# Loading 16 slots of the last V tile as two pieces of 8 in a decode attention kernel

## The chip, the cores and the metric

One core of a Trainium2 chip. The metric is the device time of one execution, in microseconds (us). The change concerns the last 4 us of some 630.

## The reference

Decode attention with grouped queries: 1 query per head, 32 query heads, 8 K/V heads, 65,536 keys, head size 128, bf16.

```python
k = jnp.repeat(k, rep, axis=1)              # rep = 32 / 8
v = jnp.repeat(v, rep, axis=1)
scores = jnp.einsum("bhqd,bhkd->bhqk", q, k) * D ** -0.5
p = _softmax(scores, axis=-1)
return jnp.einsum("bhqk,bhkd->bhqd", p, v)
```

K and V are 134 MB each and every byte is used once.

## The kernel before

K and V of a head are loaded in two tiles each, of 128 partitions x 256 "slots" (keys) x 128 values: 8 MB. The last V tile of all is loaded in ever smaller pieces, each with its own semaphore, so that little work is left when the last byte lands:

```python
TAIL = 32
CUTS = [0, 128, 192, 224, 240, 248, 252, 256]
...
    # load_v, last tile (SP issues); earlier piece, waits: cut
    for lo, hi, s in list(zip(CUTS, CUTS[1:], s_v))[1:]:
        load(v, g, b, 0, s, lo, hi)
```

TensorE multiplies slots 0 to 223 in groups of four (512 columns) into one accumulator. VectorE folds that accumulator into one row per partition (`vs`) while the last 32 slots arrive. Those are taken slot by slot (128 columns), and the folded part is added by the gather (two matmuls in the trace) before the last piece:

```python
    for t in range(SL - TAIL, SL):                 # slots 224 to 255
        if t in CUTS:
            pe.wait_ge(s_v[CUTS.index(t)], 16)
        if t == CUTS[-2]:                          # slot 252
            pe.wait_ge(s_dv, d_last)               # VectorE's fold is done
            gather(D, start=False, stop=False)
        w0 = t % PS // 4 * 32 + 16 + 4 * (t % 4)
        i = pe.matmul(
            out=fin, lhsT=et[:, 1, w0:w0 + H], rhs=io[:, t, :], start=(t == SL - TAIL),
            stop=(t == SL - 1), skip_group_check=True,
        )
    i.then_inc(s_pe, 1)                            # then ACT scales, and stores the result
```

Of the kernel before, what the change touches and what calls it, by code (L numbers as in the profile page):

```python
# [21 lines left out]
WB = 160  # L22
PS = 64
TAIL = 32
CUTS = [0, 128, 192, 224, 240, 248, 252, 256]


class Queue:
# [21 lines left out]
def kernel(  # L50
# [21 lines left out]
    def sem(name):  # L72
        return ctx.enter_context(nc.semaphore(name))
# [33 lines left out]
    s_q, s_st = sem("s_q"), sem("s_st")  # L107
    s_v = [sem(f"s_v{i}") for i in range(len(CUTS) - 1)]
    s_dv, s_ac, s_gp = sem("s_dv"), sem("s_ac"), sem("s_gp")
# [8 lines left out]
    def down(eng, which, s, n, wait=False):  # L118

        w = dict(sync_type="semaphore", id=s.num, ant_name=s.name)  # L120
        eng.add_instruction(mybir.InstEventSemaphore(  # L121
            name=nc.get_next_instruction_name(), engine=which, sync_info=mybir.SyncInfo(
                on_wait=[mybir.SyncWait(wait_mode="sem-ge-imm", wait_value=n, **w)] if wait else [],
                on_update=[mybir.SyncUpdate(update_mode="sem-sub-imm", update_value=n, **w)],
            ),
        ))
# [11 lines left out]
    def load(src, g, b, at, s, lo=0, hi=SL):  # L138
        sp.dma_start(  # L139
            out=io[:, at * SL + lo:at * SL + hi, :], in_=rows(src, g, b)[:, lo:hi, :]  # L140
        ).then_inc(s, 16)
# [13 lines left out]
    def values_done(n):  # L155
        SP.wait((s_vc, n))
        if n:
            sp.sem_inc(s_vd, 1)  # L158

    def load_v(g, b):  # L160
        done = 2 * (2 * g + b)
        if (g, b) == (G - 1, 1):
            SP.wait((s_vc, done - 1))
            load(v, g, b, 0, s_v[0], CUTS[0], CUTS[1])
            values_done(done)
            down(sp, mybir.EngineType.SP, s_v[2], 16)
            for lo, hi, s in list(zip(CUTS, CUTS[1:], s_v))[1:]:
                load(v, g, b, 0, s, lo, hi)
# [182 lines left out]
    for t in range(SL - TAIL, SL):  # L351
        if t in CUTS:
            pe.wait_ge(s_v[CUTS.index(t)], 16)
        if t == CUTS[-2]:
            pe.wait_ge(s_dv, d_last)
# [200 lines left out]
```

## Time and profile before

| | before |
|---|---|
| time, median of 3 (range) | 629.74 us (629.56 to 630.29) |
| span of the profiled run | 627.6 us |
| DMA queue, share of the 16 engines' span | 99.1% |
| TensorE, VectorE busy | 56%, 55% |

The lines behind this are shown in the prediction. The loads run for 99% of the span, so what is left to win is the time from the last loads to the end.

### The profile page before, as it was taken

Reading aid. Unit: us, or ns where it says so; the run is one execution under the profiler, and the core shown is the slowest. Engines: PE = TensorE matmul, PEld = TensorE weight load, DVE = VectorE, ACT = ScalarE, POOL = GpSimd, SP = SyncE. Lnnn points to the kernel's source line nnn. Section 1 sums busy time; section 2 is a strip of 40 time slices with the busy share of each in tenths; the row PEclk is TensorE's granted clock in tenths of the full one; section 3 lists DMA queues with packets and bytes.
Section 4 is the critical chain, followed back from the end, with each engine's and each line's share of the span. In section 5 each row is a group of like instructions: output and inputs, shape, how many; then the busy total and the mean of one; then the engine's idle time right before and its main releaser. Section 6 shows DMA issues by size and latency. Waiting matters only on the chain. (4 is left out here: it accounts for less than half of the span.)

```text
span 627.6 us, 7061 instructions
## 1 busy us (share of the span) xinstructions
PE 350.0 (56%) x2142; PEld 137.9 (22%) x2142; DVE 345.5 (55%) x154; ACT 34.4 (5%) x26; POOL 8.8 (1%) x40
## 2 busy tenths in 40 slices
PE   1865483827638275381844809458183571886344
PEld 0322131312213032130321303123031230332112
DVE  7795835649066490764807557084670946684210
ACT  0000100020000200002000020000200002000100
POOL 2000000000000000000000000000000000000000
PEclk9979696977959789596896968869698695999578
DMA  8999999999999999999999999999999999999996
GB/s 365 438 468 401 468 401 468 401 468 401 468 401 468 401 468 401 451 418 447 422 418 451 418 451 414 455 405 464 401 468 401 468 401 468 396 440 434 434 434 269
DMA packets 6859, 268.48 MB, mean 428 GB/s; under 512 B 841, under 2 KB 1097, under 8 KB 1353
## 3 DMA queue, kind: packets, MB, share of 16 engines
q1 hardware_dynamic: 6800, 268.45, 99.1%
q8 instruction: 1, 0.02, 0.0%
q10 hardware_dynamic: 56, 0.01, 0.0%
q14 instruction: 2, 0.01, 0.0%
HBM read 268.44 MB, written 0.01 MB: 428 GB/s over the span
## 5 line engine op out<-in xcount | busy, mean ns | idle before, releaser
L300 PE MATMUL acc<-io,wz 128*128 x1024 | 268.1, 412 | 190.0 <-PEq L121 160.3
L372 DVE STREAM_TRANSPOSE io<-io 128x4096 uint32<-128x4096 uint32 x64 | 279.9, 4416 | 157.8 <-DVEq L121 157.8
L300 PEld LDWEIGHTS acc<-io,wz 128*128 x1024 | 104.8, 102 | 353.4 <-issue 273.6
L253 PE MATMUL acc<-io,et 128*16 128x512 bf16 x1016 | 70.9, 409 | 20.4 <-PEq L121 19.3
L439 ACT ACTIVATE zs<-acc,nmb 128x2048 bf16<-128x2048 f32 x8 | 15.7, 1967 | 556.7 <-DVE nmb L419 556.7
L409 DVE TENSOR_REDUCE mg<-acc 128x1 f32<-128x2048 f32 x8 | 18.3, 2292 | 48.3 <-DVEq L121 48.3
L253 PEld LDWEIGHTS acc<-io,et 128*16 128x16 bf16 x1016 | 27.6, 94 | 58.5 <-issue 34.7
L247 PE MATMUL pf<-zs,sel 128*4 128x130 f32 (+1 forms) x20 | 5.7, 387 | 53.3 <-PEq L121 53.3
L375 DVE STREAM_TRANSPOSE et<-zs 128x1024 bf16<-128x1024 bf16 x17 | 20.8, 1225 | 21.9 <-SPq L158 12.1
L449 ACT ACTIVATE acc<-wz 128x2560 f32<-128x2560 bf16 (+2 forms) x8 | 16.3, 2040 | 1.0 <-ACT zs L439 0.2
L411 DVE TENSOR_REDUCE m<-pt 1x4 f32<-1x128 f32 x8 | 2.2, 279 | 22.8 <-DVEq L121 22.8
L518 POOL COPY wz<-qT 32x16 bf16<-32x16 bf16 x32 | 6.1, 189 | 513.4 <-PE acc L300 441.0
L247 PEld LDWEIGHTS pf<-zs,sel 128*4 128x4 f32 x20 | 1.2, 83 | 53.7 <-issue 53.7
L325 PE MATMUL pt<-et 128*16 128x512 bf16 x32 | 12.9, 405 | 0.0
L383 DVE TENSOR_REDUCE zs<-zs 128x128 f32<-128x512 f32 x9 | 6.1, 681 | 7.6 <-DVEq L121 7.6
L422 DVE TENSOR_TENSOR zs<-acc,sely 128x512 f32<-128x512 f32 x8 | 8.5, 1066 | 0.0
L471 DVE TENSOR_TENSOR zs<-acc,sely 128x512 f32<-128x512 f32 x1 | 0.7, 691 | 11.6 <-PE acc L253 11.6
L342 PE MATMUL pb<-ident,nrow 1*128 1x1 f32 x8 | 1.6, 199 | 7.5 <-PEq L121 7.5
L325 PEld LDWEIGHTS pt<-et 128*16 128x16 bf16 x32 | 3.1, 96 | 4.3 <-issue 1.1
L340 PE MATMUL pt<-ident,mg 128*1 128x128 f32 x8 | 2.3, 283 | 2.6 <-PEq L121 2.6
L419 DVE COPY nmb<-pb 128x1 f32<-128x1 f32 x8 | 1.3, 158 | 4.0 <-DVEq L121 4.0
L342 PEld LDWEIGHTS pb<-ident,nrow 1*128 1x128 f32 x8 | 1.2, 144 | 8.9 <-issue 8.9
(29 smaller groups left out, 21.2 us busy)
## 6 DMA issues: line engine op xcount, KB each, us to landing
io<-in_v_dram SPq DMA_DIRECT2D x5, 4096.0 KB, 16.9
io<-in_k_dram SPq DMA_DIRECT2D x8, 2048.0 KB, 27.3
io<-in_k_dram SPq DMA_DIRECT2D x2, 4096.0 KB, 34.3
io<-in_v_dram SPq DMA_DIRECT2D x1, 2048.0 KB, 10.7
io<-in_v_dram SPq DMA_DIRECT2D x1, 1024.0 KB, 12.9
io<-in_v_dram SPq DMA_DIRECT2D x1, 512.0 KB, 13.7
io<-in_v_dram SPq DMA_DIRECT2D x1, 256.0 KB, 13.9
io<-in_v_dram SPq DMA_DIRECT2D x2, 128.0 KB, 13.7
```

The source lines that it names most:

```text
L247: return pe.matmul(out=pf[0:H, 0:w], lhsT=sel[:, :], rhs=vs[:, 0:w], skip_group_check=True, **kw)
L253: return pe.matmul(out=vacc[32 * c:32 * c + 16, :, :], lhsT=et[:, ch // 2, w0:w0 + 16], rhs=io[:, PS * ch + 4 * tt:PS * ch + 4 * tt + 4, : ...
L300: i = pe.matmul(out=bass.AP(acc, r_o, [[2560, P], [1, 512]]), lhsT=bass.AP(wz, r_w + ((2 * s + e) * WB - 4 * u), [[4 * WB, P], [1, P]]), r ...
L325: pe.matmul(out=pt[0:16, :], lhsT=et[:, 0, 0:16], rhs=et[:, 0, :], start=True, stop=True)
L372: dve.transpose(out=part, in_=part).then_inc(s_kt, 2)
L375: dve.transpose(out=et[:, :, :].rearrange("p i n -> p (i n)"), in_=ex[:, 2 * b:2 * b + 2, :].rearrange("p i n -> p (i n)"),).then_inc(s_et, 1)
L383: DV.mark(dve.tensor_reduce(out=vs[:, 0:D], in_=vy[:, :, :], axis=AX.X, op=ALU.add))
L409: dve.tensor_reduce(out=mg[:, :], in_=sc, axis=AX.X, op=ALU.max).then_inc(s_mg, 1)
L422: dve.tensor_tensor(out=vy[:, :, :].rearrange("p d y -> p y d"), in0=vacc, in1=sely[:, :, None].to_broadcast([P, 4, D]), op=ALU.mult,).the ...
L439: act.activation(out=ex[:, :, :].rearrange("p b n -> p (b n)"), in_=sc, func=ACT.Exp, bias=nmb[:, :], scale=SCALE, accum_out=vs[:, D + g % ...
L449: act.activation(out=part, in_=wz[:, 0, 0:1].to_broadcast([P, part.shape[1]]), func=ACT.Copy).then_inc(s_cl, 1)
L518: gp.tensor_copy(out=wz[r, :, c0:c0 + H].rearrange("p (s w) h -> p s w h", s=2), in_=qTb[r, :, :, g, :],).then_inc(s_w, 1)
```

## The change

The intent is to let TensorE begin on slots 224 to 231 when they are there, instead of waiting for all 16.

```diff
-CUTS = [0, 128, 192, 224, 240, 248, 252, 256]
+CUTS = [0, 128, 192, 224, 232, 240, 248, 252, 256]
```

Through the loops above this adds one load, one semaphore and one wait on TensorE.

## The prediction

The sum: 629.74 - 0.13 = 629.61 us, each term from the trace or the runs of the kernel before.

> **What bounds the kernel now.** I read the page from its top down: first the shares of the span, to find the engine that is never idle, then the chain that ended last, to see what sets the end, and then the last microseconds piece by piece, since the change touches nothing else.
>
> The DMA row and the queues, from the page of the kernel before:
>
> ```profile
> span 627.6 us, 7061 instructions
> PE 350.0 (56%) x2142; PEld 137.9 (22%) x2142; DVE 345.5 (55%) x154; ACT 34.4 (5%) x26; POOL 8.8 (1%) x40
> ...
> DMA  8999999999999999999999999999999999999996
> ...
> q1 hardware_dynamic: 6800, 268.45, 99.1%
> ...
> HBM read 268.44 MB, written 0.01 MB: 428 GB/s over the span
> ```
>
> No compute engine is busy for more than 56% of the span, and the DMA row shows nines in nearly every slice. 268.4 MB of K and V are loaded once, by one queue that takes 99.1% of the 16 engines' time. So some 620 of the 627.6 us are the stream of loads, which the change leaves as it is (same bytes, same order, same addresses). Only the tail, from the arrival of the last V slots to the end, can move. Its chain of waits, in order of time (start, us, what):
>
> ```profile
> 608.12 0.43 SPq L139
> 608.55 0.04 issue
> 608.59 13.68 DMA io<-in_v_dram
> 622.27 0.04 issue
> 622.32 1.73 PE pf L358 x28
> 624.04 0.22 PE pf L247 x2
> 624.26 0.24 PE pf L358 x4
> 624.50 0.02 issue
> 624.52 0.02 ACTq L37
> 624.53 0.05 issue
> 624.59 0.36 ACT o L486
> ```
>
> The load issued at 608.59 us is the 16-slot piece (512 KB), the very one that is to be split. When it has landed, at 622.27 us, TensorE runs 28 of the 32 small matmuls of the tail without a stop, then the two gather matmuls, then the last 4. The later pieces (8, 4 and 4 slots) do not appear: their data is there before TensorE asks. So from 622.32 us on TensorE is the bound, and the start of that burst is set by the piece in question. The timeline of that stretch (start, us, engine, line, op, tile, number, idle time before) shows what TensorE did ahead of it, and that VectorE is in time:
>
> ```profile
> 621.02 0.61 PE L253 MATMUL acc<-io,et 128*16 128x512 bf16 x8 [1.15 <-DMA io<-in_v_dram]
> 621.45 0.20 PE L347 MATMUL pb<-zs,sel 128*4 128x1 f32 x2
> 622.32 1.73 PE L358 MATMUL pf<-io,et 128*4 128x128 bf16 x28 [0.66 <-DMA io<-in_v_dram]
> 622.86 0.29 DVE L479 TENSOR_TENSOR zs<-zs 128x128 f32<-128x128 f32 x1
> ```
>
> TensorE stands idle for 0.66 us before the burst; that idle time is what the change can use. VectorE's last sum, which the gather needs, ends at 622.86 + 0.29 = 623.15 us.
>
> From the trace's semaphore and packet records I took what these views merge. The last of the 16 completions of each piece came at 620.972 (slots 192 to 224), 622.271 (224 to 240), 622.959 (240 to 248), 623.317 (248 to 252) and 623.625 us (252 to 256). A packet took 159 ns at 4096 B, 84 ns at 2048 B and 47 ns at 1024 B (medians). The 28 matmuls start from 622.316 to 623.822 us: (623.822 - 622.316) / 27 = 0.0558 us apart.
>
> [...] the pieces complete in the order of their issue. So the two halves arrive one after the other, and the first half comes about half the piece's time earlier. [...] the trace has 16 completions for the 16-slot piece, spread over 0.43 us (621.845 to 622.271), and the split gives this count to each half. [...] two 2048 B packets take 168 ns where one of 4096 B takes 159. [...]
>
> **The change part by part.** The build of both kernels shows one more DMA on SP (the 16-slot piece becomes two of 8, so three 8-slot loads in a row), one more wait on TensorE (8 matmuls, wait, 8 matmuls in place of 16), and nothing else moved on any engine.
>
> *SP issue.* The issues of these pieces start 0.474 us apart (608.591, 609.065, 609.539, 610.013). One more shifts the later three and the store of the first seven groups by 0.47 us. The pieces wait some 13.7 us in the queue from issue to landing, so a later issue delays no data. Cost on the path: 0.
>
> *DMA.* An 8-slot piece takes from the landing of its predecessor 622.959 - 622.271 = 0.688 us (8 packets per engine at 84 ns, and 16 ns). Two of them take 1.376 us, where the 16-slot piece took 622.271 - 620.972 = 1.299. Everything behind is later by 0.077 us. The landings become: first half 620.972 + 0.688 = 621.660; second half 622.348; slots 240 to 248 at 623.036; 248 to 252 at 623.394; 252 to 256 at 623.702.
>
> *TensorE.* A waiting matmul starts 0.045 us after the landing (622.271 to 622.316). First half: start 621.705 (the work ahead of it ends at 621.65, so nothing holds it), 8 x 0.0558, free at 622.15. Second half: start 622.393, free at 622.84. Now TensorE has caught up with the loads, and the next piece, which it never waited for, holds it: start 623.081. The 4 of slots 248 to 252 follow without a wait (landed 623.394, wanted at 623.53). The gather would follow at 623.081 + 12 x 0.0558 = 623.751; its own wait is for slots 252 to 256, free at 623.702 + 0.045 = 623.747, a dead heat, and VectorE's sum has been there since 623.15.
>
> *Sum.* The gather started at 623.877 before, and starts at 623.751 after: 0.126 us sooner. What follows it (two gather matmuls, 4 matmuls, the scaling on ACT, the store) is unchanged. Of the 0.611 us by which the first matmul starts sooner, 0.485 us is given back in waits for the second half and for slots 240 to 248. 629.74 - 0.13 = 629.61 us, or 0.02%.
>
> **The rivals.** First, TensorE stays the bound and the whole 0.61 us is won (629.13 us). For it: before, no wait lies inside the burst. Against it: 8 matmuls take 0.45 us and an 8-slot piece 0.69, so the loads are the slower side as soon as TensorE starts early. It could be so only at half the granted clock, at which a matmul would take about twice 0.0558, or 0.11 us, and 8 of them 0.89 us. The profile gives 0.50 from 613 to 617 us and 1.00 from 618 on, so runs in which the low clock lasts longer would be slower in both kernels, and gain more from the split.
>
> Second, the smaller pieces delay the last landing enough that the gather waits for it and the gain is gone: 629.74 us or a little more. The last landing had 623.823 - 623.625 = 0.2 us to spare before. The computed delay of 0.077 does not use that up. If a split cost 0.3 us in place of 0.077, the gather would start at 623.97, or 0.1 us later than before: 629.84 us.
>
> Third, the extra issue holds up the queue: at worst 0.47 us, so 630.2 us. Against it stand the 13.7 us of queueing. The first 2048 B packet of the tail begins at 621.265 us, 12.2 us after its issue.
>
> Fourth, the gain is real but drowned by the differences between runs: the three of before spread over 0.73 us (629.56 to 630.29), almost six times the gain. This is what I expect of the plain times.
>
> **Range and chances.** The point is 629.6 us. All mechanisms together give 629.1 to 630.2. The spread between runs, and a possible other chip for the changed kernel, which I cannot know, widen it: 629.0 to 630.4. A change of over 2% would be 12.6 us, and the whole tail from the last landing to the end of the span is 627.6 - 623.6 = 4.0 us. So within 2% has 0.99, and the rest is halved between the sides, for something that I do not see.
>
> **What would show it.** In the trace after: matmuls of the tail in three bursts, 8, 8 and 16 with the gather in between, each started by a landing; landings 0.69 us apart three times; the chain of waits passing through a later load, slots 240 to 248 or 252 to 256, in place of the first piece; the gap from the landing of slots 192 to 224 to the gather matmul down from 623.877 - 620.972 = 2.905 us to about 2.78. Wrong would be: a burst of 32 without a wait from the first half on (the first rival), a gather that starts later after that landing than 2.905 us (the second), or a gap between the landings before slots 224 (the third).

## The result, and the profile after

| | before | after |
|---|---|---|
| median of 6 runs | 630.01 us | 629.49 us |
| range | 629.43 to 631.23 | 629.32 to 630.30 |
| ratio | | 0.9991 (95%: 0.9978 to 1.0004) |
| span of the profiled run | 627.6 us | 627.8 us |

Ratios here are the mean time of one kernel's runs over that of the other's in the same rounds, so not quite the ratio of the medians. Executions over 1.5% slower than the fastest of the same kernel are left out of the means. The interval includes 1: timing alone shows no difference. The spread of each kernel's own runs is several times the predicted gain of 0.13 us.

The page of the kernel after, DMA row and load queue. The stream of loads is as before; the queue has 144 packets more (128 for the split, 16 for its completions):

```profile
DMA  8999999999999999999999999999999999999996
...
q1 hardware_dynamic: 6944, 268.45, 99.1%
```

The end of its chain of waits (start, us, what):

```profile
608.60 12.41 DMA io<-in_v_dram
621.00 0.04 issue
621.05 1.02 PE acc L253 x5
622.07 0.02 PE pb L347
622.10 1.84 PE pf L358 x28
623.94 0.32 PE pf L247 x2
624.26 0.24 PE pf L358 x4
```

This is not the predicted chain: it runs through the load that ends at 621.00, which is slots 192 to 224, and then stays on TensorE. The windows of the same trace (columns: window, its length, busy time of PE, PEld, DVE, ACT, POOL, then granted clock, DMA share, GB/s) tell why TensorE was behind at first. The granted clock is the share of TensorE's full clock that the profile records:

```profile
620.50:622.00 1.50, 1.40 (x16) 0.38 (x12) 0.00 (x0) 0.00 (x0) 0.00 (x0) 0.50 1.06 396
622.00:623.20 1.20, 1.20 (x24) 1.08 (x19) 1.03 (x2) 0.00 (x0) 0.00 (x0) 0.86 0.91 305
```

The clock was at half until 622.34 us, so the work ahead of the tail took 1.02 us in place of 0.61. The records of single instructions show, however, that TensorE had caught up before the end. It finished slot 239 early and started slot 240 at 623.110, 0.043 after that piece landed (623.067). The gather started at 623.880, 0.043 after the last landing (623.837). A view that joins neighbouring instructions of one line into one piece hides such short waits. In this trace the gather began 2.875 us after slots 192 to 224 had landed. Before it was 2.905, and 2.78 was predicted. So the gain was 0.03 us here, because the last landing came 0.10 later than worked out (2.832 us after slots 192 to 224, against 2.730; the expectation of e2 below has 0.11). One of its 16 completions was late: the fifteenth came at 623.715, the last at 623.837. The span is 0.23 us longer than before all the same, for a reason behind the tail: from ACT's store to the end it took 2.82 us in this trace, where it was 2.60 before and 2.61 and 2.60 in the two later traces of the changed kernel (e2, e5).

### The profile page after: what moved, and what is told of

It reads as the page before. It is cut to its first block, busy times and chain, and to the rows that moved or that the text cites. A ratio compares the mean times of both kernels' runs of the same rounds, so it can differ in the third digit from the quotient of the medians.

```text
span 627.8 us, 7062 instructions
## 1 busy us (share of the span) xinstructions
PE 354.6 (56%) x2142; PEld 139.1 (22%) x2142; DVE 345.5 (55%) x154; ACT 34.4 (5%) x26; POOL 8.8 (1%) x40
## 3 DMA queue, kind: packets, MB, share of 16 engines
q1 hardware_dynamic: 6944, 268.45, 99.1%
## 5 line engine op out<-in xcount | busy, mean ns | idle before, releaser
L300 PE MATMUL acc<-io,wz 128*128 x1024 | 271.0, 417 | 187.2 <-PEq L121 157.5
L253 PE MATMUL acc<-io,et 128*16 128x512 bf16 x1016 | 72.4, 416 | 19.3 <-PEq L121 19.2
L204 DVE MEMSET acc<- 128x2560 f32 x1 | 2.2, 2192 | 1.6 <-SPq L64 1.6
```

Of the source, the lines that this page charges most:

```text
L253: return pe.matmul(out=vacc[32 * c:32 * c + 16, :, :], lhsT=et[:, ch // 2, w0:w0 + 16], rhs=io[:, PS * ch + 4 * tt:PS * ch + 4 * tt + 4, : ...
L300: i = pe.matmul(out=bass.AP(acc, r_o, [[2560, P], [1, 512]]), lhsT=bass.AP(wz, r_w + ((2 * s + e) * WB - 4 * u), [[4 * WB, P], [1, P]]), r ...
```

## The experiments

All times below count from the **base**, the last completion of slots 192 to 224. This takes out what the stream of loads did before. A landing is the last of a load's 16 completions. "Tail end" is the end of the last matmul of the tail. Landings, gather and tail end come from the trace's records of semaphores and instructions:

| kernel | clock in the tail | first piece | last landing | gather | tail end |
|---|---|---|---|---|---|
| before | full | 1.299 | 2.653 | 2.905 | 3.510 |
| before, again (e1) | falls at 2.23 | 1.290 | 2.637 | 3.488 | 4.545 |
| after | half to 1.34, then full | 0.687 | 2.832 | 2.875 | 3.480 |
| after, again (e2) | full | 0.687 | 2.690 | 2.759 | 3.364 |
| after, third (e5) | full | 0.692 | 2.685 | 2.764 | 3.368 |
| split, one wait (e3) | full | 0.699 | 2.741 | 3.068 | 3.673 |
| 24, 4, 4 (e8) | full | 1.906 | 2.579 | 3.511 | 4.115 |
| 32 (e4) | falls at 2.74 | 2.479 | 2.479 | 5.304 | 6.322 |
| after, gather ahead (e6) | half to 1.98, then full | 0.687 | 2.727 | 2.985 | 3.590 |
| eight of 4, gather ahead (e7) | full | 0.375 | 2.876 | 2.505 | 3.333 |
| 8, 8, 4, 4, 4, 4 (e9) | full | 0.668 | 2.784 | 2.387 | 3.215 |
| after, padded SP (e10) | full | 0.691 | 2.706 | 2.755 | 3.360 |
| after, more matmuls (e11) | full | 0.677 | 2.703 | 2.756 | 3.361 |
| 12, 8, 4, 4, 4, more matmuls (e12) | full | 0.979 | 2.688 | 2.402 | 3.230 |

The theory at the start: the tail ends when TensorE has worked off what lands late, so it matters when the pieces land, the end gains 0.13 us, and all else is noise. The rivals: the cuts do not matter, or the later landings take the gain back.

### e1 and e2: both kernels once more

No edit. Is the first trace of the changed kernel typical?

> The kernel before, for a second trace. All times here count from the last of the 16 completions of slots 192 to 224 (called the base). First trace of before: landings at 1.299 (slots 224 to 240), 1.987, 2.345, 2.653 us; gather matmul at 2.905; end of the last tail matmul at 3.51. Theory: the landings repeat to 0.03 us, and at full granted clock the gather is at 2.90. If the clock is granted at half as the base arrives (as in the trace of the changed kernel), still 2.90 as long as it is back at full when the 16-slot piece lands. Rival (a delayed last landing is chance): a last landing over 2.70 appears here too. It would cost nothing, since the last landing had 0.2 us to spare.

> The changed kernel, for a second trace, times from the base as before. First trace of it: landings 0.687, 1.365, 2.062, 2.414, 2.832; gather at 2.875, freed by the last landing, which came 0.11 us later than the prediction's 2.730 because 1 of its 16 completions was late; end of the last tail matmul 3.48. Theory A (the late completion is a collision with the fetch of instructions of 16 KB that runs on one engine from about 2.2 us after the base in both traces): the fetch starts again at 2.15 to 2.25, one of the 16 completions is late by 0.05 to 0.2, and the gather is at 2.82 to 2.95. Rival B (chance of that one run): the last landing is at 2.73 to 2.76 and the gather at 2.78, 0.13 before that of the kernel before.

Measured: 630.51 us for the kernel before, 629.29 for the changed one, single runs on one chip, so of unknown state. The chain of the second trace of the changed kernel:

```profile
609.55 13.54 DMA io<-in_v_dram
623.10 0.04 issue
623.14 0.83 PE pf L358 x12
623.97 0.22 PE pf L247 x2
624.19 0.24 PE pf L358 x4
```

This is the predicted chain. It runs through the load of slots 240 to 248, landed at 623.10; 12 matmuls follow (8 and 4), then the gather and the last 4. The gather was at 2.759, predicted 2.78. The late completion did not come back (last landing at 2.690), and the fetch of instructions began 1.99 us after the base. So my theory A, in which that fetch collides with the last piece each time, fell; rival B held. The start of the fetch does not decide it in the other traces either: it began 2.20 us after the base in the first trace of the kernel before and 2.24 in e7, and the last completion came 0.01 and 0.03 behind the fifteenth; at 2.18 in e10 it came 0.17 behind, with a last landing of 2.706. The first trace's late completion was chance, or has a cause that I did not find.

The second trace of the kernel before repeats the landings of the first to 0.02 us and starts its tail at 1.334 (1.344 in the first). It also shows where 1 us can go. Its last burst in its chain, and its windows:

```profile
622.34 2.36 PE pf L358 x28
```

```profile
622.00:623.20 1.20, 0.86 (x16) 0.86 (x17) 1.13 (x4) 0.00 (x0) 0.00 (x0) 1.00 0.88 287
623.20:624.50 1.30, 1.30 (x17) 1.30 (x15) 0.05 (x1) 0.00 (x0) 0.00 (x0) 0.51 0.00 0
```

The burst has the same 28 matmuls, but 2.36 us in place of the 1.73 shown in the prediction. The clock fell to half at 623.24 us, in the middle of the burst, and the matmuls then came 0.107 us apart in place of 0.056. The tail end moved from 3.51 to 4.545, by 1.03 us, and this run was 630.51. The nine runs of the kernel before on that chip fall into two groups, six at 629.47 to 629.65 (called the lower level below) and three at 630.44 to 630.53 (the upper level). Nothing in the code differs. The expectation of 2.90 for the gather at full clock is therefore not tested by this run. The first trace of the changed kernel has the same two spacings in one burst: 0.107 us from 622.018 to 622.338, at half clock, and 0.056 from 622.402 on, at full. Before the fall in e1 the clock was full for 6.83 us. What makes it fall, no trace here shows.

### e3: the split load without its use

```diff
-        if t in CUTS:
+        if t in CUTS and t != 232:
             pe.wait_ge(s_v[CUTS.index(t)], 16)
+        if t == 224:
+            pe.wait_ge(s_v[CUTS.index(232)], 16)
```

> The piece is split, but TensorE waits for both halves ahead of slot 224. Only the cost of the split load is left, without its use. Theory (split costs 0.07 us, the start decides the end): first tail matmul at 1.365 + 0.045 = 1.41 in place of 1.344, one burst of 28, gather at 1.41 + 28 x 0.0558 = 2.97, 0.07 later than in the kernel before; end of the last tail matmul 3.58. A last landing at 2.83 + 0.045 is still ahead of it. Rival (the last landing sets the end whatever the start): gather at 2.87 to 2.90 as in the changed kernel. Time within 0.3 us of the kernel before, not resolved by single runs.

Measured: 629.62 us, a single run. The timeline of the tail's matmuls:

```profile
622.45 1.72 PE L360 MATMUL pf<-io,et 128*4 128x128 bf16 x28 [0.82 <-DMA io<-in_v_dram]
```

There is one burst of 28 again, and a tail end of 3.673, which is 0.163 later than before. Of that, the later landing of both halves is 1.373 - 1.299 = 0.074 us, as predicted (0.077). The other 0.09 was not: the matmul started 0.135 after the landing in place of 0.045. The two waits in a row may be why; no run tests that. The last landing was there 0.33 us before the gather started, so the rival that it alone sets the end is out. Split without an earlier start, the piece costs time.

### e4 and e8: fewer cuts

```diff
-CUTS = [0, 128, 192, 224, 232, 240, 248, 252, 256]
+CUTS = [0, 128, 192, 224, 256]              # e4; its gather stays at slot 252
+CUTS = [0, 128, 192, 224, 248, 252, 256]    # e8
```

> The opposite of the change, as far as it goes: slots 224 to 256 loaded as one piece. Theory (TensorE's burst starts when the first piece has landed, and the burst then runs without a stop): landing at about 2.6 us after the base (32 slots in 8 packets per engine of 8192 B, 313 ns each, are 2.5 us), first matmul at 2.62, gather 28 x 0.0558 later at 4.2, end of the last tail matmul at 4.8, so 1.3 us later than in the kernel before: about +1.3 us, ratio 1.0021. Rival (only the last landing counts, and how it is cut does not): no change, ratio 1.000.

> Slots 224 to 248 in one piece of 24, then two of 4: half of the way to the one piece of 32. Theory: first landing at about 1.95, burst from 2.0, gather at 2.0 + 28 x 0.0558 = 3.56, end of the last tail matmul 4.16, 0.65 after the kernel before at full clock; if the clock falls in the burst up to 1.7 more. Time: lower level about 630.2, median 630.2 to 631.5, ratio 1.001 to 1.003, between the kernel before and the one piece of 32 (1.003). Rival (the cuts do not matter while the last piece is small): ratio 1.000.

Measured: e4 632.21 us (630.71 to 632.37), ratio 1.003 (1.0017 to 1.0044). e8 630.20 us (630.06 to 631.72), ratio 1.001 (0.9996 to 1.0023). The tails, e4's first (timeline):

```profile
623.52 2.99 PE L358 MATMUL pf<-io,et 128*4 128x128 bf16 x28 [1.84 <-DMA io<-in_v_dram]
```

```profile
623.34 1.73 PE L358 MATMUL pf<-io,et 128*4 128x128 bf16 x28 [1.26 <-DMA io<-in_v_dram]
```

TensorE's idle time before the burst is 1.84 and 1.26 us, where the kernel before had 0.66. The tail of e8 ends 0.605 later than that of the kernel before, against 0.65 expected. That of e4 was caught with the clock falling during the burst (2.99 us for 28 matmuls), so its size is not the one expected at full clock. Of its five runs, four lie at 631.89 to 632.37 and one at 630.71, which is 1.1 to 1.2 us above the lower level of the kernel before, near the expected 1.3. That this one had full clock is likely, but it has no trace. The sign is timed beyond noise in e4, with the fall of the clock in it: the cuts matter. That the start of the burst sets the end is read from e8's trace, at full clock, and from e4's, where the last landing is the earliest of all (2.479) and the tail end the latest.

### e5 and e6: the changed kernel timed, and with the gather ahead

e5 has no edit. The edit of e6 lets a late last landing hold up only its own 4 matmuls:

```diff
+        if t == CUTS[-2]:
+            pe.wait_ge(s_dv, d_last)
+            gather(D, start=False, stop=False)
         if t in CUTS:
             pe.wait_ge(s_v[CUTS.index(t)], 16)
-        if t == CUTS[-2]:
-            pe.wait_ge(s_dv, d_last)
-            gather(D, start=False, stop=False)
```

> The changed kernel, timed in five rounds beside the next two, with a third trace. So far the runs of the kernel before lie on two levels, 629.47 to 629.65 and 630.44 to 630.53 us, and its second trace had the clock fall to half at 623.24, within the last burst, whose matmuls then came 0.107 apart in place of 0.056. Theory: the spread of the runs is where this fall happens to lie; the changed kernel has the same two levels, its lower one 0.1 to 0.2 us under that of the kernel before (about 629.4 against 629.55); ratio 0.999 to 1.000. In the trace: landings 0.69, 1.36, 2.06, 2.41, 2.69 to 2.84 after the base; at full clock, gather at 2.76 to 2.88. Rival (a split of the piece is worth more than the tail shows): a lower level at 629.2 or less.

> The changed kernel with the gather issued ahead of the wait for the last piece, so that a late last landing holds up only the last 4 matmuls. Theory: at full clock the gather starts at 2.06 + 0.045 + 12 x 0.0558 = 2.78 whatever the last landing, the last 4 matmuls at 3.00 (last landing at 2.83 at the worst, 2.88 with the wait), end of the last tail matmul at 3.38, as in the second trace of the changed kernel (3.364) and 0.1 before its first one (3.48). Time: within 0.1 us of the changed kernel, not resolved. Rival (the late completion in the first trace of the changed kernel did not cost anything): no difference to it in a trace with a late completion either, 3.48.

Measured: e5 629.28 us, the median of five runs (four at 629.25 to 629.33 and one of 630.63), ratio 0.9995 (0.9982 to 1.0009); a run of 670.26, at a granted clock of 0.553, is left out. The kernel before on that chip: six runs at 629.47 to 629.65, and 630.07, 630.44, 630.48, 630.53. So both kernels seem to have two levels, with one run between them; the lower one of the changed kernel is some 0.27 us under that of the kernel before (means), somewhat more than expected, and I do not know why. The trace repeats e2: gather at 2.764, tail end 3.368.

e6 took 629.57 us (629.22 to 630.22), ratio 0.9995 (0.9982 to 1.0009), which is not told apart from e5. Its trace fell into a run with half clock until 1.98 us after the base, TensorE was behind all along, and the tail ended at 3.590. It settles nothing about the late landing.

### e7 and e9: finer cuts

```diff
-CUTS = [0, 128, 192, 224, 232, 240, 248, 252, 256]
+CUTS = [0, 128, 192, 224, 228, 232, 236, 240, 244, 248, 252, 256]    # e7
+CUTS = [0, 128, 192, 224, 232, 240, 244, 248, 252, 256]              # e9
```

In both, the gather stands ahead of the wait for slot 248.

> Slots 224 to 256 in eight pieces of 4, and the gather ahead of slot 248. Theory (TensorE starts as early as the data is there, then waits for each piece, and the end is the last landing and 4 matmuls): landings 0.34 to 0.36 apart, the last at 8 x 0.35 = 2.78; 4 matmuls of 0.223 fit between them at full clock; the gather at 2.3 to 2.5; the last 4 start at 2.83, end of the last tail matmul 2.83 + 3 x 0.0558 + 0.219 = 3.21, 0.3 before the kernel before and 0.15 before the changed one. At half the clock (0.107 a matmul, 0.43 for 4) TensorE is the bound from the first landing on: end at about 0.4 + 32 x 0.107 + 0.43 + 0.2 = 4.4. Time: lower level about 629.25, ratio 0.9993 to 1.000. Rival (more issues and smaller packets cost more than they give): a last landing at 2.95 or later, end 3.4 or later.

> Slots 224 to 256 as 8, 8, 4, 4, 4, 4, and the gather ahead of slot 248: one load more than the changed kernel, where the eight pieces of 4 had three more. Theory: landings 0.69, 1.37, 1.73, 2.09, 2.43, 2.76 after the base; at full clock TensorE keeps up, the last 4 matmuls start at 2.80, end of the last tail matmul 3.19, 0.17 before the changed kernel (3.365). Rival (the end of the program, which came 0.46 us late on SP in the kernel of eight pieces, depends on the number of SP's instructions and takes the gain back): the same end of the tail, but from ACT's store to the end of the span 3.1 in place of 2.6, and a time of 629.6 or more. If the rival is wrong: a lower level of 629.1 to 629.2.

Measured: e7 629.83 us (629.74 to 630.17), ratio 0.9999 (0.9986 to 1.0013). Its tail ends at 3.333 where 3.21 was expected: the 4-slot pieces landed up to 0.386 us apart. The last landing, 2.876 in place of 2.78, did not set this end. The gather started at 2.505, when TensorE was through with slots 244 to 247 (landed at 2.239), and the last 8 matmuls followed it without a wait, the last 4 from 2.946 on. Even so its tail is no longer than that of the changed kernel, yet its median is 0.55 above that of e5's fast runs. As one piece the same 32 slots (1 MiB) had landed at 2.479 (e4), so as eight of 128 KB they came 0.40 later. On SP, the first eight issues from the 64-slot piece on took 0.33 to 0.43 us each in e7, and the ninth and tenth 2.29 and 2.72 us; the cause is not shown. The pieces of those two landed 0.34 and 0.30 us after the ones before them, no later than the pieces ahead. e9 took 629.48 us (629.41 to 630.59), ratio 0.9996 (0.9982 to 1.0009). Its tail ends at 3.215, 0.15 before the changed kernel, as expected, yet its lower level (629.41 to 629.65, on another chip) lies no lower. Both lost time behind the tail. From the start of ACT's store to the end of the span the changed kernel (e2) takes 627.5 - 624.9 = 2.6 us, e7 628.1 - 624.9 = 3.2, and e9 2.8, less than the 3.1 of its rival.

### e10: three more instructions on SP, no more loads

```diff
             for lo, hi, s in list(zip(CUTS, CUTS[1:], s_v))[1:]:
                 load(v, g, b, 0, s, lo, hi)
+            for _ in range(3):
+                sp.sem_inc(s_pad, 1)           # nothing waits for it
```

> The changed kernel with three semaphore increments that nothing waits for on SP, behind the last load: as many more instructions on SP as the three more loads of the eight pieces, but no loads. Theory (the late end of the kernel of eight pieces comes of SP's instructions, not of its loads): from ACT's store to the end of the span 3.1 in place of 2.6, lower level 629.7 in place of 629.3. Rival (it comes of the loads): 2.6, and the time of the changed kernel.

Measured: 629.86 us (629.76 to 629.98), ratio 0.9997 (0.9983 to 1.0011). Its tail is that of the changed kernel (3.360). The last line of ACT in the timelines, and the span in the pages, of e2:

```profile
624.90 0.51 ACTq L488 DMA_DIRECT2D out_dram<-o  x1
```

```profile
span 627.5 us, 7062 instructions
```

and of e10:

```profile
624.98 0.51 ACTq L491 DMA_DIRECT2D out_dram<-o  x1
```

```profile
span 628.1 us, 7065 instructions
```

From the store to the end it is 2.6 us in the first and 3.1 in the second, and the runs are 0.5 us slower than those of e11, which were taken beside them, without any load more. In the records, SP's closing instructions wait: the second of its last three DRAIN instructions took 125 ns and came 0.42 us after the one ahead of it, where in e2 it took 7 and came 0.065 after. e7 shows the same to the digit. SP has 83 instructions in the traces of e7 and e10, 80 in all traces of the changed kernel, and 76 to 80 in those without the delay. In e9 it has 81, and the last of the three is the one that takes 124 ns and comes late, by about 0.36 us. Counted from SP's first instruction in the trace, the late one is the 80th in all three kernels; in the changed kernel the 80th is SP's last. So the wait goes with the place in SP's instruction stream, and the changed kernel ends right at that place. My guess was a fetch of instructions, but the records do not bear it out: e10's DMA packets of kind "instruction" after 624 us begin at 624.59, 627.53 and 628.17, none of them in the gap from 626.48 to 626.90, and in e7 and e9 none begins in the gap either. So the place is shown and the cause of the wait stays open.

### e11: more work for TensorE

```diff
             if ch in (1, 2):
-                pe.matmul(out=pt[0:16, :], ...)        # an unused product
+                for _ in range(3):
+                    pe.matmul(out=pt[0:16, :], ...)
```

> The changed kernel with three useless matmuls of 512 columns in place of one, behind the second and the third quarter of each V tile, so that TensorE is busy for some 0.9 us more of the two stretches (617.3 to 618.5 and 619.9 to 621.0) in which it waits for V at the end. Theory (the spread of the runs of one kernel is the granted clock of the tail[...]): the upper level (630.4 to 630.6) is gone or rarer, all runs at 629.2 to 629.5; the tail in the trace at full clock, gather at 2.76. Rival (the levels have another cause): as many runs at the upper level as before. It may also be slower by up to 1 us, if the clock is at half as the extra matmuls run, which would then hold up the first half of the piece.

Measured: 629.36 us (629.31 to 629.82), ratio 0.9991 (0.9977 to 1.0004). Four of five runs lie at 629.31 to 629.39, none at 630 or more; the kernel before on that chip had four of nine at 630 or more. The mean granted clock of the traced run is 0.826, where it is 0.807 to 0.815 in the three traces of the changed kernel. Two of the changed kernel's 12 other runs (the slow one left out) were at 630 or more, so five runs do not prove that the level is gone. Nor does the trace test it: its tail, 3.361, is that of e2, which had full clock without the extra matmuls. That they bear on the clock of the tail was my guess, and is not shown.

### e12: what the experiments point to

```diff
-CUTS = [0, 128, 192, 224, 232, 240, 248, 252, 256]
+CUTS = [0, 128, 192, 224, 236, 244, 248, 252, 256]
```

with the gather ahead of slot 248 (as in e7) and the useless matmuls of e11. It has as many loads as the changed kernel, so as many instructions on SP.

> What the experiments point to, in one kernel: five pieces as in the changed kernel (no more instructions on SP), but of 12, 8, 4, 4 and 4 slots, the gather ahead of slot 248, and the useless matmuls[...]. Theory: landings 1.02, 1.70, 2.06, 2.41, 2.72 after the base; at full clock TensorE starts at 1.07 and has the gather behind it at about 2.6, end of the last tail matmul 3.2 to 3.25, 0.13 before the changed kernel; from ACT's store to the end of the span 2.6. Lower level 629.15 to 629.25 (changed kernel 629.25 to 629.33), none or one of the five at 630.4 or more, median 629.2, ratio to the kernel before 0.9985 to 0.9995. Rival (the fewer waits of the first piece cost as much as the later ones gain): end at 3.36 and no better than the changed kernel.

Measured: 629.27 us (629.26 to 629.56), ratio 0.999 (0.9977 to 1.0004). The end of its chain:

```profile
610.07 12.06 DMA io<-in_v_dram
622.13 0.04 issue
622.18 1.54 PE pf L359 x24
623.72 0.22 PE pf L247 x2
623.93 0.46 PE pf L359 x8
```

The gather now stands before the last 8 matmuls, and the tail ends at 3.230, 0.13 before the changed kernel, as expected; from the store to the end it is 2.6 us again. Which share of the 0.13 is the cuts' and which the place of the gather no run separates. The lower level was expected at 629.15 to 629.25; the lowest run is 629.26. With e11's, 10 runs with the extra matmuls had none at 630 or more; the kernel before on e12's chip had two of nine. The five runs of e12 have the lowest median of the kernels timed, but it is not shown to be faster than the changed kernel: they ran on different chips, the fastest runs are the same (629.26 and 629.25), and in its one trace the base itself lay 0.12 us later than in e5's.

## Why the prediction was right

- **What bounds the kernel, and that only the tail can move.** Right. The stream of loads kept its 99.1%, and even one piece in place of the five of the changed kernel (e4) moved the time by 0.3%.
- **The issue on SP costs nothing.** Right as to the data: in e2 the issues still come 0.474 us apart and no piece landed late. What the prediction did not see is that the number of instructions on SP has a price elsewhere (three more cost 0.5 us in e10). With one more load than the changed kernel has, e9 took 2.8 us from the store to the end in place of 2.6.
- **The split delays what is behind it by 0.077 us.** Right, if a little large: 0.066, 0.057 and 0.056 in the three traces, from the landings of the second half (1.365, 1.356, 1.355) against 1.299.
- **TensorE catches up and then waits for slots 240 to 248.** Right in e2 and e5, at full clock. The piece landed at 2.047 and 2.052 after the base (2.064 predicted), and the chain passes through it. In the first trace it also waited there, though the chain does not show it.
- **The sum, 0.126 us.** At full clock the tail end moved from 3.510 to 3.364 and 3.368, so 0.14 to 0.15; e10 and e11, with the same tail, have 3.360 and 3.361. On the side of before this rests on one trace at full clock. In the first trace of the changed kernel it was 0.03, because the last landing was late by 0.10. The prediction had called the race between the gather and the last landing a dead heat, so a late landing was bound to show. Its cause stays open: the collision that I proposed was not borne out by e2.
- **The time.** 629.61 worked out, 629.49 measured. The agreement is partly luck, since the median of six runs depends on how many lie on the upper level.
- **The fourth rival, a gain drowned by the runs.** Right, and one trace tells of something that they drown in: the moment at which the clock falls (e1, 1.03 us). That the whole upper level comes of this is not shown.
- **A remark that stays open:** that runs with a longer low clock would gain more from the split. No trace has the kernel before with half clock ahead of its burst, so the comparison has to be worked out. With half clock to 1.34, as in the first trace of the changed kernel, the kernel before would lose next to nothing, since its burst starts at 1.344; the gain there was 0.03, not more. With half clock to 1.98, as in e6, its matmuls would be 0.107 in place of 0.056 us apart for 0.63 us, a loss of some 0.3 us by my estimate, so that it would end near 3.8; e6, which also has the gather ahead, ended at 3.590. In the times, the one run of the upper level in e5 (630.63) is not lower than those of the kernel before (630.44 to 630.53).

## What to carry to other kernels

Where a kernel is one long stream of loads, the last pieces are best cut, as far as these traces show, so that the consumer never has more work left than the time until the next landing (at full clock the tail ended at 4.115 with 24 slots at once in e8, and at 3.215 with e9's cuts). Starting earlier by 0.6 us gains only the part by which the consumer was behind at the end, here 0.14. Differences of this size are read from traces, measured from a landing near the end, and not from run times, whose spread (here in part, by one trace, from the clock granted in the tail: 1.03 us in e1) is several times larger. Added instructions on an engine that seems free can cost time at the end of the program: three cost 0.5 us here (e10).
